# FFT convolution and spectral mixing on one core: the first transform by channel halves of one sequence, four copies of x on GpSimd, later loads, and a filter turned for two ticks at once

## The chip, the core and the metric

The kernel runs on one core of a Trainium2 chip. The metric is device time in microseconds for one launch; the median of three runs before the change is 372.04 us (372.01 to 373.72). The engines are TensorE (PE in the profile; PEld is its loading of weights), VectorE (DVE), ScalarE (ACT), GpSimd (POOL, which also issues DMAs whose f32 data is turned into f16 on the way) and SyncE (SP, which issues the other DMAs). Every engine works through its own instructions in order; engines meet at semaphores.

## What is computed

`x` has 8 sequences of 5696 positions and 128 channels, `h` one filter of 5696 positions for each channel. Each sequence is convolved with the filter, and the result goes through a spectral mixing step and a small gate:

```python
Yf = rfft(x, n=2*S, axis=1) * rfft(h, n=2*S, axis=0)[None]
x1 = irfft(Yf, n=2*S, axis=1)[:, :S, :]            # first part
X = rfft(x1, axis=1)[:, :64]                       # second part: 64 modes
Y = X mixed over channels by w_r + i*w_i, zero elsewhere
u = x1 + irfft(Y, n=S, axis=1)
out = u + relu(u @ w_ch)                           # float32
```

## The kernel before

The position is split as 64 q + p, with q from 0 to 88 (NQ = 89) and p from 0 to 63 (J = 64). The sequences are taken in four pairs. For each pair the convolution's transform has two steps, then comes the product with the filter, then the way back.

*First transform* (`a_tile`). `Xin` holds x with q on the partitions. For one channel, a matmul with the 128 columns (b, p) of the two sequences as weights and the table `F` (line 143) as the moving operand gives 180 columns: real and imaginary part for 90 frequencies k. A tile is four channels in two PSUM banks; its evacuation, scaled by 1/64, writes `As` with (b, p) on the partitions. 32 tiles make a pair. Which engine evacuates is set by lists: `SHARE` for the first pair, a turn of ACT and DVE for others, "both" for the last tile.

*Second transform* (`second`). For each k, matmuls of 64 rows each, one for each b, turn p into the second frequency, with tables `M`. A *tick* is four frequencies; there are NT = 23 ticks. The result is copied to `Xs` by ACT (`copied`) or read straight from PSUM by DVE, and DVE multiplies it with the filter into `U` (`products`), 2048 columns wide (4 x 512: two parts of the filter, two sequences, four k of 128 channels). Two ticks later (LC = 2) PE takes `U` times `Wc`, ACT copies to `Zs`, and SP stores `Zs` to memory; three ticks later (LM = 3) `modes` multiplies `Zs` with `G` for the spectral part. Tick 0 of a pair is handled apart: `second(g, 0, 0, d)` does the first 116 or 120 channels as soon as their tiles are in `As`, the rest follows, and three calls of `first_u` make its product.

*The filter.* h goes through the same first transform once (line 441: 16 tiles, `Hp` to `Ah`), with idle-time matmuls on `F` and on `Hp`, `F` between them (lines 448 to 452; their results are not used). `filter_tick` makes the second transform of four frequencies of h, evacuates it into `Hs`, and two DMAs on SP copy each half of the partitions to the other half ("turned", line 508), because the product needs both. Six filter ticks (LH = 6) stand among the first pair's tiles, the others run in the ticks of pair 0, six ahead. `filter_tick` also issues the loads of `G` at t = 1, 3, 5, 7, 9, 11.

*Loading x.* For the first pair, POOL issues 6 DMAs for h, 14 for x into `Xr`, then 6 for `M`; DVE copies x from `Xr` into `Xin` in eight pieces (`x_place`, line 364) between the evacuations of `Ah`. `Xr` lies where `Hs` will be, so `Hs` waits for these copies. For the second pair four pieces are loaded into `Xh` ahead of the first pair's tiles (line 739) and four into `Xt` in ticks; DVE places them at ticks `XPLACE`. At the border of two pairs the first six tiles of the next pair stand between the last ticks, then 26 tiles follow (line 764).

After the last pair the stored `Zs` come back, the way back from frequencies is done by matmuls with `S4` and `IBs`, and the gate and the stores of the output follow (from line 773 on).

All operations are recorded by helpers, so most rows of the trace have one line number: 323 for every matmul, 320 for every DMA, 313 and 317 for scaled evacuations by ACT and DVE, 311 and 315 for plain ones, 652 for products, 623 for those of tick 0, 365 for `x_place`. Tiles tell them apart.

Of the kernel before, what the change touches and what calls it, by code (L numbers as in the profile page):

```python
# [123 lines left out]
def bass_long_conv_fft__then__afno_spectral_mix_kernel(nc, x, h, moe_w_r, moe_w_i, moe_w_ch, out):  # L124
# [17 lines left out]
    f1 = np.zeros((P, 2 * NK))  # L142
    f1[0:NQ] = np.stack([fwd.real, fwd.imag], axis=2).reshape(NQ, 2 * NK)
# [71 lines left out]
    AW, HW, GW = NK * 2 * D, NK * D, (NK // 2 + 1) * P  # L215
    a_as = take(AW * 2)
    a_sb = at("As", AW, F16, a_as)
    XS = D + 2
    XW = 2 * J * XS
# [14 lines left out]
    DH = D // 2  # L234
    HS = DH + 2
# [7 lines left out]
    KH = [NK - 2 * XN, NK - XN]  # L243
    x_h = [at(f"Xh{i}", XB, F16, a_h + (i % 2 * HW + KH[i // 2] * D) * 2) for i in range(NXH)]
# [4 lines left out]
    f1_sb = at("F1", 2 * NK, F16, take(2 * NK * 2))  # L249
# [9 lines left out]
    a_h2, a_xt = a_h + HW * 2, a_x + 4 * S + 2 * B * P  # L259
    a_as1, a_m2 = a_as + 2 * S, a_m + 4 * S  # L260
    zt_off = [(a_h, a_h2), (a_as1, a_as1 + 2 * ZP), (a_as1 + 4 * ZP, a_as1 + 6 * ZP), (a_h + 2 * ZP, a_h2 + 2 * ZP),
# [9 lines left out]
    o_big = [a_h + 4 * ZP, a_h2 + 4 * ZP, a_st + 4 * S] + [a_g + 2 * ZP + 4096 * i for i in range(2)] + \  # L271
            [a_xt + 4096 * i for i in range(2)]
    o_off = [a_h + 4 * ZP + 4096, a_h2 + 4 * ZP + 4096, a_m2 + 2 * ZP + 4 * P, a_st + 4 * S + 4096]
# [73 lines left out]
    R.add("scalar", lambda e: e.copy(zf, ap(f1_sb, 2 * NK, J, P - J, 1, [[0, XW // 2]])), [("f1",)], [("xz",)])  # L347
# [16 lines left out]
    def x_place(i, src, toks):  # L364
        R.add("vector", lambda e: e.tensor_copy(bass.AP(x_sb, i * XN * XS, [[XW, NQ], [XS, XN], [1, D]]),  # L365
                                                src),
              list(toks) + XZ, [("xin", i)])
# [18 lines left out]
    def next_rows(c_):  # L386
        dma("gpsimd", bass.AP(x_all, QA * RA + c_ * XB, [[RA, 8], [XC * XB, 2], [1, XB]]),
            bass.AP(x.tensor, x.offset + QA * ROW + c_ * XB, [[ROW, 8], [S * D, 2], [1, XB]]), "x", (),
            [("xr", c_, 0), ("xr", XC + c_, 0)])

    def last_row(i):
        o_, w_ = i * XC // 2 * XB, XC // 2 * XB
        dma("gpsimd", bass.AP(x_all, (QA + 8) * RA + o_, [[RA, 1], [XC * XB, 2], [1, w_]]),
            bass.AP(x.tensor, x.offset + (QA + 8) * ROW + o_, [[ROW, 1], [S * D, 2], [1, w_]]), "x", (), [("xl", i)])

    for c_ in range(XC):
        if c_ == XC - 1:
            next_rows(c_)
        first_rows(0, c_)
        if c_ < XC - 1:  # L400
            next_rows(c_)
        first_rows(1, c_)
        if c_ in (0, 1):
            last_row(c_)
    XZ = [("xz",)]
    XIN = [("xin", i) for i in range(2 * XC)]
    XR = [[("xr", i, p_) for p_ in range(2)] + [("xl", i % XC // 2)] for i in range(2 * XC)]
# [19 lines left out]
    ZSLOT, DA, DF = 6, 116, 120  # L427
    ZBANK = [4, 5, 6]
    MB = 7
    WARM, LONG = 92, 22  # L430


    for i in range(WARM):
        mm(pv(6 + i % 2, 0, [[1, 2 * NK]]), f1_sb[:, 0:P], f1_sb[:, :], True, True, [("f1",)], [bank(6 + i % 2)])
# [6 lines left out]
    for j in range(16):  # L441
        t = turns("h", [0, 2, 4])
        for i in range(4):
            d = 4 * j + i
            mm(pv(t + i // 2, (i % 2) * 2 * NK, [[1, 2 * NK]]),
               ap(hp_sb, 2 * J * HS, 0, P, d, [[HS, 2 * J]]), f1_sb[:, :], True, True,
               [("hz",), ("hp", d // DC), ("f1",)], [bank(t + i // 2)])
        for i in range(4 if j < 15 else 0):
            mm(pv(6 + i % 2, 0, [[1, 2 * NK]]), f1_sb[:, 0:P], f1_sb[:, :], True, True, [("f1",)], [bank(6 + i % 2)])
# [3 lines left out]
        evac(bass.AP(ah_sb, 4 * j, [[HW, P], [DH, 2 * NK], [2, 2], [1, 2]]),  # L453
             pv(t, 0, [[1, 2 * NK], [512, 2], [2 * NK, 2]]),
             [bank(t), bank(t + 1)], [("ah", j)], 1.0 / 64,
             eng="vector" if j in (3, 7) else "scalar")
        if j % 2:
            i = j // 2 % 2 * XC + j // 4
            x_place(i, bass.AP(x_all, i * XB, [[RA, NQ], [D, XN], [1, D]]), XR[i])

# [4 lines left out]
    def a_tile(j, slots, eng=None):  # L465
        t = turns("s", slots) if len(slots) > 1 else slots[0]
        for i in range(4):
            d = 4 * j + i
            mm(pv(t + i // 2, (i % 2) * 2 * NK, [[1, 2 * NK]]),
               ap(x_sb, XW, 0, P, d, [[XS, 2 * J]]), f1_sb[:, :], True, True,  # L470
               XIN + XZ + [("f1",)], [bank(t + i // 2)])
        if eng == "both":
            for i, e in enumerate(("vector", "scalar")):
                evac(bass.AP(a_sb, 4 * j + 2 * i, [[AW, P], [D, 2 * NK], [1, 2]]), pv(t + i, 0, [[1, 2 * NK], [2 * NK, 2]]),
                     [bank(t + i)], [("as", j + i)], 1.0 / 64, eng=e, after=once(("hp", j), HP))
            return
        evac(bass.AP(a_sb, 4 * j, [[AW, P], [D, 2 * NK], [2, 2], [1, 2]]),
             pv(t, 0, [[1, 2 * NK], [512, 2], [2 * NK, 2]]),
# [10 lines left out]

    def filter_tick(t, banks):  # L490
        n = len(ticks[t])
        hb = banks
        for i, k in enumerate(ticks[t]):
            for r in range(2):
                for dh in range(2):
                    mm(pv(hb[dh], i * DH, [[1, DH]]),
                       ap(m_sb, MW, J * dh, J, k * 3 * J + (J if r == 0 else 0) + dh * J, [[1, P]]),
                       ap(ah_sb, HW, J * dh, J, (2 * k + r) * DH, [[1, DH]]), r == 0, r == 1,
                       AHT + mtok(k) + [("ag", k)], [bank(hb[dh])])
        lo, hi = KT * t * D, (KT * t + n) * D  # L500
        old = once("xr", [t_ for r_ in XR for t_ in r_]) if t == 0 else []
        for i in range(NXH):
            if KT * t + n > KH[i // 2]:
                old = old + once(("xh", i), xtok(i))
        evac(h_sb[:, lo:hi], pv(hb[0], 0, [[DH, n], [512, 2], [1, DH]]), [bank(hb[0]), bank(hb[1])], [("h", t, 0)],
             eng="scalar" if t < LH + 2 and t != 2 else "vector",
             after=old)
        for p0, p1 in ((0, J), (J, 0)):
# [457 lines left out]
```

## Time and profile before

| | |
|---|---|
| median of three runs | 372.04 us |
| span of the profiled execution | 370.1 us |
| TensorE busy | 354.7 us |
| ScalarE busy | 316.2 us |
| VectorE busy | 291.8 us |
| GpSimd busy | 75.2 us |
| first matmul on `Xin` | 27.33 us |
| first product of pair 0 | 43.43 us |

The profiled execution's own time is its span of 370.1 us, from its first to its last instruction; the device time of the runs is measured around the whole launch. A row of the timeline has start, duration, engine, line, operation, output and inputs, count, and in brackets the idle time of the engine before it with what released it. Rows of several instructions are merged, and their duration is that from first start to last end. A row of groups ends in busy time and mean ns of one, then the idle time before. A row of the DMA view ends in the size of one transfer and the median us from issue to landing. The end of a matmul is modelled, so starts are the safer figures on PE.

### The profile page before, as it was taken

The page shows a single profiled execution, that of the slowest core. Times are in us where ns is not written, and L with a number is a line of the kernel's source. Part 1 is how long each engine was busy: PE and PEld are TensorE (multiplying, and loading weights), DVE is VectorE, ACT ScalarE, POOL GpSimd, SP SyncE. Part 2 cuts the span into 40 slices and gives each one's busy share as a digit, 9 for nine tenths or more (in the row PEclk, how much of TensorE's full clock was granted, in tenths as well). Part 3 has the DMA queues.
Part 4 walks back from the last instruction along what each step waited for, and adds up shares of the span by engine and source line. Part 5 has one row for each costly group of instructions (what it writes and reads, how often), then busy time and mean ns, then how long its engine had stood idle before and what let it go on. Part 6 is the DMA issues. An engine that isn't in the chain of part 4 may idle for free.

```text
span 370.1 us, 12455 instructions
## 1 busy us (share of the span) xinstructions
PE 354.7 (96%) x5350; PEld 276.5 (75%) x5350; DVE 291.8 (79%) x332; ACT 316.2 (85%) x499; POOL 75.2 (20%) x117
## 2 busy tenths in 40 slices
PE   7999899999999999999999999999999999999994
PEld 7878766667866668866668766668899888888873
DVE  3549899988999999989999988775357777756666
ACT  8559999999999999999999999995467777688885
POOL 8804012100833311823213001151000000000000
PEclk9999999999999999999999999999999999999999
DMA  7999979969999996999996999999999999999878
GB/s 139 209 271 382 249 165 292 232 198 283 93 140 213 263 258 186 132 160 215 263 278 128 171 310 363 342 345 388 381 410 386 413 410 408 418 399 376 326 291 349
DMA packets 87048, 103.94 MB, mean 281 GB/s; under 512 B 22730, under 2 KB 72522, under 8 KB 83438
## 3 DMA queue, kind: packets, MB, share of 16 engines
q1 hardware_dynamic: 64610, 81.33, 62.5%
q0 software_dynamic: 22384, 21.83, 35.4%
q8 instruction: 42, 0.69, 0.7%
q14 instruction: 12, 0.10, 0.1%
HBM read 70.61 MB, written 51.12 MB: 329 GB/s over the span
## 4 chain that ended last, share of the span: by engine, by line
PE 78%; ACT 10%; DMA 7%; DVE 3%; issue 1%; POOL 1%; DVEq 0%; POOLq 0%
PE ps L323 78%; ACT As L313 6%; DMA out_dram<-O 5%; DMA Hin<-in_h_dram 2%; ACT R L898 1%; DVE As L317 1%; ACT Xs L311 1%; DVE U L623 1%; POOL Hin L320 1%; ACT UT L311 1%; DVE O L899 0%; ACT Zs L311 0%; DVE Hp L438 0%; ACT C L313 0%; DVE Hs L315 0%
## 5 line engine op out<-in xcount | busy, mean ns | idle before, releaser
L652 DVE TENSOR_TENSOR U<-Xs,Hs 128x2048 f16<-128x2048 f16 (+1 forms) x72 | 85.8, 1197 | 12.1 <-ACT Xs L311 11.5
L323 PE MATMUL ps<-U,Wc 128*128 128x512 f16 (+1 forms) x368 | 93.8, 376 | 1.4 <-DVE U L623 1.4
L311 ACT CAST Xs<-ps 128x1024 f16<-128x1024 f32 (+1 forms) x76 | 75.0, 995 | 5.8 <-PE ps L323 3.1
L311 ACT CAST Zs<-ps 128x512 f16<-128x512 f32 (+1 forms) x132 | 70.1, 605 | 0.7
L899 DVE TENSOR_TENSOR O<-ps,R 128x512 f32<-128x512 f32 x81 | 52.4, 684 | 21.6 <-ACT R L898 11.4
L898 ACT ACTIVATE R<-ps 128x512 f32<-128x512 f32 (+1 forms) x92 | 50.5, 592 | 8.5 <-PE ps L323 8.4
L317 DVE TENSOR_SCALAR As<-ps 128x720 f16<-128x720 f32 x64 | 53.1, 879 | 4.8 <-PE ps L323 3.3
L323 PE MATMUL ps<-As,M 64*128 64x128 f16 (+3 forms) x1504 | 52.5, 214 | 2.4 <-ACT As L313 1.2
L313 ACT ACTIVATE As<-ps 128x720 f16<-128x720 f32 (+1 forms) x68 | 48.2, 771 | 5.0 <-PE ps L323 4.8
L323 PE MATMUL ps<-F,Xin 128*128 128x180 f16 x512 | 52.1, 249 | 0.1
L323 PE MATMUL ps<-WI,UT 128*128 128x256 f16 x360 | 50.8, 278 | 0.5 <-ACT UT L311 0.4
L311 ACT CAST UT<-ps 128x712 f16<-128x712 f32 x46 | 34.5, 752 | 19.4 <-PE ps L323 18.4
L323 PEld LDWEIGHTS ps<-U,Wc 128*128 128x128 f16 x368 | 29.1, 97 | 28.2 <-DVE U L623 1.9
L323 PEld LDWEIGHTS ps<-F,Xin 128*128 128x128 f16 x512 | 45.2, 155 | 6.7 <-DVE Xin L365 0.9
L323 PEld LDWEIGHTS ps<-As,M 64*128 64x128 f16 x1504 | 42.2, 94 | 8.7 <-ACT Xs L311 1.9
L323 PEld LDWEIGHTS ps<-WI,UT 128*128 128x128 f16 x360 | 38.9, 152 | 3.2 <-issue 1.8
L323 PE MATMUL ps<-IBs,C 128*128 128x356 f16 x128 | 39.2, 314 | 0.8 <-DVE O L899 0.7
L320 POOL DMA_DIRECT2D Xt<-in_x_dram x40 | 21.4, 540 | 76.5 <-PE ps L323 76.0
L323 PEld LDWEIGHTS ps<-G,Zs 128*128 128x128 f16 x512 | 26.1, 96 | 14.1 <-ACT Zs L311 0.2
L652 DVE TENSOR_TENSOR U<-ps,Hs 128x2048 f16<-128x2048 f32 (+1 forms) x16 | 35.5, 2216 | 0.0
L323 PE MATMUL ps<-G,Zs 128*128 128x128 f16 (+2 forms) x512 | 31.9, 192 | 0.1
L311 ACT CAST Zt<-ps 128x512 f16<-128x512 f32 x52 | 29.1, 659 | 0.0
(76 smaller groups left out, 479.4 us busy)
## 6 DMA issues: line engine op xcount, KB each, us to landing
out_dram<-O SPq DMA_DIRECT2D x39, 512.0 KB, 10.5
zscr<-Zs SPq DMA_DIRECT2D x62, 256.0 KB, 6.7
zscr<-Zt SPq DMA_DIRECT2D x26, 256.0 KB, 6.6
Xt<-in_x_dram POOLq DMA_DIRECT2D x20, 320.0 KB, 6.9
W<-wscr SPq DMA_DIRECT2D x4, 1024.0 KB, 8.5
ZT0a<-zscr SPq DMA_DIRECT2D x4, 1024.0 KB, 11.0
M<-cM POOLq DMA_DIRECT2D x5, 720.0 KB, 17.6
ZT1a<-zscr SPq DMA_DIRECT2D x3, 1024.0 KB, 11.1
```

The lines of the kernel that those rows point to most:

```text
L311: R.add(e, lambda h_: h_.copy(dst, src), reads, writes, after=after)
L313: R.add(e, lambda h_: h_.activation(dst, src, COPY, scale=scale), reads, writes, after=after)
L317: R.add(e, lambda h_: h_.tensor_scalar_mul(dst, src, scale), reads, writes, after=after)
L320: R.add(eng, lambda h_: h_.dma_start(dst, src), reads, writes, ring=ring, after=after)
L323: R.add("tensor", lambda h_: h_.matmul(o, l, r, start=st, stop=sp), reads, writes)
L623: R.add("vector", lambda e: e.tensor_tensor(bass.AP(u_s[0], b * 512 + d0, [[2048, P], [1024, 2], [D, n], [1, d1 - d0]]), bass.AP(s_[0], s_ ...
L652: R.add("vector", lambda e: e.tensor_tensor(uv, src, hv, MULT), bk + [("h", t, 0), ("h", t, 1, 0), ("h", t, 1, J)], [("u", i)])
L898: R.add("scalar", lambda e: e.activation(rv, src_r, RELU), bk, [("r", i % NR)], after=once(("r", i % NR), G_ALL + XTT + [("y", 0), ("y", 1 ...
L899: R.add("vector", lambda e: e.tensor_tensor(ov, src_u, rv, ADD), bk + [("r", i % NR)], [key + (h_,)], after=once(key, old))
```

## The change

- `Xin` and `As` are laid out anew. A tile of the first transform takes four channels of each channel half of *one* sequence: 128 columns are (half, p), so tiles 0 to 15 are the first sequence and 16 to 31 the second. In the first pair a tile asks only for its own sequence's pieces (`first_pair`). In `second`, the two matmuls of a frequency are now the two channel halves; a result has the bank by half and both sequences beside each other.
- The two columns that are always zero (imaginary part of k = 0 and of k = 89) are dropped: 178 columns instead of 180, and one matmul pair less at these frequencies.
- Tick 0 of a pair is split by sequence: `second(g, 0, (0,))`, its product from PSUM, then `second(g, 0, (1,))`, a copy by ACT and its product. The two sit in banks 6, 7 and 4, 5.
- x's first DMAs come sequence by sequence, 12 instead of 14. DVE places the first sequence's four pieces during the filter's tiles; the second sequence's four pieces are copied by GpSimd, behind the DMAs that it issues.
- The filter's first transform: 2 idle-time matmuls a tile instead of 4, 4 long ones instead of 22; DVE evacuates six of the sixteen tiles instead of two.
- The six filter ticks of the first pair stand behind tiles 19, 21, 23, 25, 27, 29 instead of 11, 14, 17, 20, 23, 26.
- `Hs` is laid out for two ticks at a time from tick 6 on, and one pair of DMAs turns two ticks.
- The four loads into `Xh` move from ahead of the tiles to behind the products of ticks 0, 0, 1 and 2 of pair 0; the first placing moves from tick 3 to 4. `G` is loaded at filter ticks 5, 6, 7, 8, 9, 11.

```diff
-    f1 = np.zeros((P, 2 * NK))
+    NF = 2 * NK - 2
+    f1 = np.zeros((P, NF))
...
-    def x_place(i, src, toks):
-        R.add("vector", lambda e: e.tensor_copy(bass.AP(x_sb, i * XN * XS, [[XW, NQ], [XS, XN], [1, D]]),
+    def x_place(i, src, toks, eng="vector"):
+        R.add(eng, lambda e: e.tensor_copy(bass.AP(x_sb, i // XC * 2 * XH + i % XC * XN * HS, [[XW, NQ], [HS, XN], [XH, 2], [1, DH]]),
...
+    for b_ in range(2):
+        for c_ in range(XC):
+            first_rows(b_, c_)
+            if c_ == 0:
+                next_rows(b_)
+                last_row(b_)
...
-    ZSLOT, DA, DF = 6, 116, 120
+    ZSLOT = (6, 4)
...
-    WARM, LONG = 92, 22
+    WARM, LONG = 92, 4
...
-        for i in range(4 if j < 15 else 0):
+        for i in range(2 if j < 15 else 0):
...
-             eng="vector" if j in (3, 7) else "scalar")
-        if j % 2:
-            i = j // 2 % 2 * XC + j // 4
+             eng="vector" if j in (2, 4, 6, 9, 11, 14) else "scalar")
+        if j % 4 == 3:
+            i = j // 4
...
-    def a_tile(j, slots, eng=None):
+    def a_tile(j, slots, eng=None, first_pair=False):
+        b_ = j // 16
+        xin = XIN[b_ * XC:b_ * XC + XC] if first_pair else XIN
...
-               ap(x_sb, XW, 0, P, d, [[XS, 2 * J]]), f1_sb[:, :], True, True,
-               XIN + XZ + [("f1",)], [bank(t + i // 2)])
+               ap(x_sb, XW, 0, P, d // DH * 2 * XH + d % DH, [[HS, 2 * J]]), f1_sb[:, :], True, True,
+               xin + XZ + [("f1",)], [bank(t + i // 2)])
...
+        couple = LH <= t < NT - 1
+        if not couple or t % 2:
+            us = (t - 1, t) if couple else (t,)
+            lo = h_at(us[0])[0]
+            for p0, p1 in ((0, J), (J, 0)):
+                dma("sync", bass.AP(h_sb, p0 * 2 * HW + lo + 2 * dw, [[2 * HW, J], [1, 2 * dw]]),
+                    bass.AP(h_sb, p1 * 2 * HW + lo, [[2 * HW, J], [1, 2 * dw]]), "s", [("h", u, 0) for u in us], [("h", u, 1, p0) for u in us])
+        if t in GTICK:
...
+    GTICK = [max(LH - 1 + i, 2 * i + 1) for i in range(NG)]
...
+            product(g_, t, (ps, sl[0], 4096), bk[0], (0,))
+            second(g_, 0, (1,))
+            evac(bass.AP(x_s[e], 256, [[1024, P], [512, 2], [1, n]]), pv(ZSLOT[1], 256, [[512, 2], [1, n]]), bk[1], [("xs", e)], eng="scalar")
+            product(g_, t, (x_s[e], 0, 1024), [("xs", e)], (1,))
...
-    XPLACE = [3, 5, 7, 9, 11, 14, 17, 20], [9, 10, 13, 14, 17, 18, 20, 22]
+    XPLACE = [4, 5, 7, 9, 11, 14, 17, 20], [9, 10, 13, 14, 17, 18, 20, 22]
...
+                for e in range(NXH):
+                    if t == (0, 0, 1, 2)[e]:
+                        x_load(1, e, x_h[e], xtok(e), [("u", t)] + [t_ for r_ in XR for t_ in r_])
...
-    for i in range(NXH):
-        x_load(1, i, x_h[i], xtok(i), [t_ for r_ in XR for t_ in r_])
...
+    HTICK = [19, 21, 23, 25, 27, 29]
     for j in range(32):
-        a_tile(j, FOUR, "both" if j == 31 else SHARE[j])
-        if j >= 11 and j % 3 == 2 and (j - 11) // 3 < LH:
+        a_tile(j, FOUR, "both" if j == 31 else SHARE[j], True)
+        if j in HTICK:
             h_ = turns("s", FOUR)
-            filter_tick((j - 11) // 3, [h_, h_ + 1])
-    second(0, 0, 0, DF)
+            filter_tick(HTICK.index(j), [h_, h_ + 1])
+        if j % 4 == 1 and j < 16:
+            i = XC + j // 4
+            x_place(i, bass.AP(x_all, i * XB, [[RA, NQ], [D, XN], [DH, 2], [1, DH]]), XR[i], "gpsimd")
+    second(0, 0, (0,))
```

More of the change, by code (lines that the diff above doesn't have):

```diff
@@ L493, in filter_tick @@
         for i, k in enumerate(ticks[t]):
-            for r in range(2):
+            sk = slots(k)
+            for n_, slot in enumerate(sk):
+                r = (slot + 1) % 2 if k else 0
                 for dh in range(2):
@@ L621, in first_u @@
-    def first_u(b, s_, row, tok, d0, d1):
-        n = len(ticks[0])
-        R.add("vector", lambda e: e.tensor_tensor(
-            bass.AP(u_s[0], b * 512 + d0, [[2048, P], [1024, 2], [D, n], [1, d1 - d0]]),
-            bass.AP(s_[0], s_[1] + d0, [[row, P], [0, 2], [D, n], [1, d1 - d0]]),
-            bass.AP(h_sb, d0, [[2 * HW, P], [HW, 2], [D, n], [1, d1 - d0]]), MULT),
-              [tok, ("h", 0, 0), ("h", 0, 1, 0), ("h", 0, 1, J)], [("u", 0)])
+            sk = slots(k)
+            for n_, slot in enumerate(sk):
+                r = (slot + 1) % 2 if k else 0
+                for dh in range(2):
+                    col = k * 3 * J + (J if r == 0 else 0) + dh * J
+                    mm(pv(sl + dh, bs[0] * 256 + i * DH, [[256, nb], [1, DH]]),
+                       ap(m_sb, MW, J * dh, J, col, [[1, P]]),
+                       ap(a_sb, AW, J * dh, J, slot * D + bs[0] * DH, [[1, nb * DH]]), n_ == 0, n_ == len(sk) - 1,
+                       rd + mtok(k), [bank(sl + dh)])
@@ L766, in bass_long_conv_fft__then__afno_spectral_mix_kernel @@
                 if j == 31:
[L767 removed]
+                    second(g_ + 1, 0, (0,))
                 if wp and j % 2 == 1:
```

162 lines of the change are left out of this document (72 added, 90 removed).

## The prediction

> **What bounds the kernel now.** First the page, for busy shares; then windows by stage, to see which engine fills each; then the timeline of the first 43 us and the chain of waits over time, to see what ends each stage.
>
> ```profile
> span 370.1 us, 12455 instructions
> PE 354.7 (96%) x5350; PEld 276.5 (75%) x5350; DVE 291.8 (79%) x332; ACT 316.2 (85%) x499; POOL 75.2 (20%) x117
> ```
>
> ```profile
> 3.00:24.00 21.00, 20.19 (x221) 19.41 (x220) 9.95 (x11) 16.07 (x15) 14.02 (x24) 1.00 1.02 201
> 24.00:35.00 11.00, 10.93 (x123) 8.49 (x121) 8.16 (x11) 7.32 (x12) 4.15 (x8) 1.00 1.02 400
> 13.27:27.33 14.06, 14.03 (x146) 11.92 (x147) 8.05 (x11) 9.72 (x14) 3.75 (x6) 1.00 1.06 245
> 27.33:42.82 15.49, 14.93 (x226) 12.79 (x225) 13.70 (x17) 14.04 (x22) 4.15 (x8) 1.00 1.04 329
> 104.90:141.00 36.10, 36.10 (x559) 23.26 (x560) 34.46 (x30) 35.17 (x58) 8.33 (x16) 1.00 1.07 228
> ```
>
> Columns: window, length, busy time of PE, PEld, DVE, ACT, POOL, granted clock, DMA share, GB/s. The ticks (104.90 to 141) are full on PE, 36.10 of 36.10, with ACT close behind. From 13.27 to 27.33 PE is full too, but not with work that the result needs:
>
> ```profile
> 11.98 2.37 DVE L438 COPY Hp<-Hin 89x4096 f16<-89x4096 f16 x2 [6.71 <-DMA Hin<-in_h_dram]
> 13.27 0.53 PE L323 MATMUL ps<-F,Hp 128*128 128x180 f16 x4 [0.78 <-DVE Hp L438]
> ...
> 13.84 2.10 ACT L313 ACTIVATE Ah<-ps 128x720 f16<-128x720 f32 x3 [4.00 <-PE ps L323]
> ...
> 13.95 0.48 PE L323 MATMUL ps<-F,Hp 128*128 128x180 f16 x4
> 14.26 0.47 PE L323 MATMUL ps<-F 128*128 128x180 f16 x4
> ...
> 16.30 0.90 DVE L317 TENSOR_SCALAR Ah<-ps 128x720 f16<-128x720 f32 x1
> ...
> 19.07 5.41 ACT L313 ACTIVATE Ah<-ps 128x720 f16<-128x720 f32 x8 [0.47 <-PE ps L323]
> 19.28 0.68 DVE L365 COPY Xin<-Xr 89x2048 f16<-89x2048 f16 x1
> 22.56 0.69 DVE L365 COPY Xin<-Xr 89x2048 f16<-89x2048 f16 x1 [2.60 <-DMA Xr<-in_x_dram]
> 23.22 4.27 PE L323 MATMUL ps<-Hp,F 128*128 128x344 f16 x22
> 26.33 0.69 DVE L365 COPY Xin<-Xr 89x2048 f16<-89x2048 f16 x1 [0.81 <-DMA Xr<-in_x_dram]
> ...
> 27.33 4.68 PE L323 MATMUL ps<-F,Xin 128*128 128x180 f16 x48
> 27.84 6.24 DVE L317 TENSOR_SCALAR As<-ps 128x720 f16<-128x720 f32 x7 [0.82 <-PE ps L323]
> 28.15 4.25 ACT L313 ACTIVATE As<-ps 128x720 f16<-128x720 f32 x6 [3.67 <-PE ps L323]
> ...
> 41.27 1.96 ACT L313 ACTIVATE As<-ps 128x720 f16<-128x720 f32 x3
> ```
>
> The groups on F alone and the 22 on Hp,F are filler that writes nothing used. The filter's own transform ends near 23.2; x's transform starts at 27.33 because it asks for all eight pieces of x and the eighth lands at 26.33. So the DMA ends this stage (share 1.02, 201 GB/s while f32 is turned into f16). At a pair's border the end is set otherwise:
>
> ```profile
> 95.26 7.47 ACT As L313 x11
> 102.78 0.37 PE ps L323 x8
> ...
> 103.78 0.70 DVE U L623
> ...
> 104.58 0.27 DVE U L623
> ...
> 104.90 43.31 PE ps L323 x644
> ```
>
> Evacuations by ACT, then second, the copy, two products of tick 0, and PE is the bound again at 104.90. There are three such borders.
>
> **The change, part by part.** *x of one sequence first.* A tile now takes 4 channels of each half of one sequence, so tiles 0 to 15 need only four pieces. Half of x was in by 19.28: that copy is the fourth, and it waited for no DMA (the first four pieces are two of each sequence, the same bytes as one whole sequence; x's transfers go from 14 to 12 with the same bytes). What then ends the stage is DVE, which gets six of the sixteen evacuations of Ah (two before) besides four pieces of x. Its queue: the evacuation of tile 2 can begin when PE has done three groups of four with two fillers each. Four matmuls take 14.26 - 13.95 = 0.31, so six take 0.47, and tile 2 is ready near 13.27 + 0.94 + 0.57 = 14.8 (0.57 from the first matmul at 13.27 to its evacuation at 13.84). Then 6 x 0.90 + 4 x 0.69 = 8.15, to 22.9. PE needs 16 x 0.31 + 30 x 0.078 + 4 x 0.194 = 8.1, to 21.4; ACT 10 x 0.68 = 6.8 (5.41 / 8 each), to 20.6; both are covered. From the last copy to the first matmul on x it is 27.33 - 27.02 = 0.3. x's transform starts at 23.2 instead of 27.33: **-4.1 us**. The cut filler (4 to 2 per tile, 22 to 4) costs nothing, as it only filled that wait; if the granted clock, 1.00 in every window, fell for want of it, that would show at once. M follows x in the same queue at 400 GB/s, so its first piece (737 KB of six) is in by some 28, before the first filter tick.
>
> *GpSimd's four copies.* The trace shows no copy on POOL. The nearest rows:
>
> ```profile
> L540 POOL MEMSET ZT0b<- 32x2048 uint32 x1 | 1.8, 1794 | 21.0 <-DVE U L652 21.0
> L365 DVE COPY Xin<-Xr 89x2048 f16<-89x2048 f16 x8 | 5.4, 686 | 5.6 <-DMA Xr<-in_x_dram 5.6
> ```
>
> POOL writes 2048 elements per partition in 1.79. A copy that streams reads beside writes takes that, one that does them in turn 3.6; I take 2.0, near the row, as one pass. The bounds are 1.8 and 3.6. The second sequence lands between about 22.0 (first quarter, from 22.56) and 26.33; four copies end at 22.0 + 8.0 = 30.0, with 0.3 to PE 30.3 (POOL's DMA issues before them are over by 17, as the window from 13.27 shows 3.75 us of them and nothing after). Tile 16 is due when eight evacuations by DVE are nearly through: 23.2 + 0.5 + 8 x 0.89 (6.24 / 7) - 1.2 for the four bank pairs in flight = 29.6. **+0.7 us** of waiting, with 0 and +7.1 at the bounds; each 0.1 us of a copy is 0.4 us.
>
> The Trainium skill, "GPSIMD Engine Reference", section 3.1, gives 1.03 cycles per element where the ports bind and about 1.8 for a tight software loop, at 1.2 GHz: by the page an estimate of 1.8 or 3.1 us for 2048 elements. The memset's 1794 ns agrees with the first; no row here shows the second; by it the sum below would come to about nothing.
>
> *The filter's ticks later.* They move from tiles 11 to 26 to tiles 19 to 29, behind the copies whose memory Hs overwrites. Before, ACT had 14.04 us of work in 15.49. Now its first 16 tiles hold 8 x 0.71 (4.25 / 6) = 5.7 us of ACT against 7.1 of DVE, and all the five Hs copies come after: 8 x 0.71 + 5 x 0.59 + 0.5 = 9.1 in the second half. 7.1 + 9.1 + 0.5 to start is 16.7, against 15.9 from 27.33 to the end of its evacuations at 43.23; the four bank pairs and the wait for tile 16 let ACT catch some up: **+0.3**, bounds 0 and +0.8.
>
> ```profile
> L311 ACT CAST Hs<-ps 128x512 f16<-128x512 f32 x7 | 4.1, 589 | 0.0
> ...
> L313 ACT ACTIVATE As<-ps 128x720 f16<-128x720 f32 x64 | 46.6, 787 | 5.0 <-PE ps L323 4.8
> L311 ACT CAST Zs<-ps 128x512 f16<-128x512 f32 x124 | 67.7, 619 | 0.7
> ```
>
> *Turned for two ticks; next x and G later.* Turning in couples takes 16 of SP's 46 transfers of Hs away and no work from PE. Its early transfers landed late while the next pair's x moved:
>
> ```profile
> Hs<-Hs SPq DMA_DIRECT2D x4, 64.0 KB, 9.3
> ...
> Hs<-Hs SPq DMA_DIRECT2D x4, 64.0 KB, 2.6
> ...
> G<-cG SPq DMA_DIRECT2D x1, 256.0 KB, 4.0
> ...
> 48.90 0.69 PE L323 MATMUL ps<-G,Zs 128*128 128x128 f16 x8
> ...
> Xt<-in_x_dram POOLq DMA_DIRECT2D x1, 320.0 KB, 6.0
> ...
> 51.51 1.21 DVE L652 TENSOR_TENSOR U<-Xs,Hs 128x2048 f16<-128x2048 f16 x1
> ```
>
> 9.3 is for issues at 36.8 to 39.7, 2.6 for those at 46.5 to 49.6. The turned filter of tick 0 is issued some 5 us before its product, so it fits by the second and not by the first; moving next x behind the product of tick 0 makes the second likely. G's first part comes out of SP after the sixth filter tick, near 40.5, and lands near 45 (4.0 and the issue); the modes that read it follow the last evacuation (41.27 + 1.96 = 43.23 before, 40.1 after) as before by 48.90 - 43.23 = 5.7, at 45.8. Its margin is under 1 us. Next x: tick 0's product ends near 42 (40.1 and the 0.37, 0.59 and 0.70 of a border with their hops); POOL then issues two transfers of 0.5 us per piece with only later loads queued behind them, and the first piece lands at 42.5 + 6.0 = 48.5 or later. DVE asks for it ahead of tick 4's product, which was at 51.51 and comes to 48.4. Behind DVE's wait stand the products, for which PE waits two ticks later. **+0.5 us** for both, bounds 0 and +2.
>
> *Borders.* Product and second of tick 0 split by sequence instead of by channel: the leftover of 0.27 and the hops about it go (104.90 - 104.48 = 0.4). ACT, 35.17 of 36.10 busy just behind, gives part back: 3 x -0.35 = **-1.05**, bounds 0 and -1.3. The first product now takes 1024 elements out of PSUM where it took 928; DVE does it while ACT still evacuates and copies, so 0. The modes now wait for both halves of a Zs, but come a tick after them: 0. The four matmuls fewer per pair (two rows of zeros gone) are 0.1 us each pair, left out. Rows of 178 instead of 180 columns: 720 to 712 elements take 1.1% off 7.47 at three borders and off some 11 us of the first: **-0.3**.
>
> *Shapes.* A product's filter is read in runs of 256 instead of 512, a Zs copy writes runs of 64 instead of 128, x is placed in runs of 64. As is written in runs of 2 at 787 / 720 = 1.09 ns per element, Zs in runs of 128 at 1.21: short runs are not dearer. 0; if a Zs copy lost 2%, ACT's slack of 0.93 in 36.10 would still cover most of it (36 such copies in the window, 0.4 us).
>
> Sum: -4.1 + 0.7 + 0.3 + 0.5 - 1.05 - 0.3 = **-3.95**. On the profiled execution the span of 370.1 becomes 366.15; the median of the runs, 372.04, lies 1.94 above that span for what surrounds it, so 368.1.
>
> **Rivals.** *Slow copies (the other side).* If POOL needs 3.6 per copy, tile 16 waits until 22.0 + 14.4 + 0.3 = 36.7, 6.4 us more than in the sum: 374.5. For it: no copy on POOL is in the trace, and all 16 tiles of the second sequence hang on the fourth. Against: 1.79 for as many elements written. It decides from 3.0 us per copy (2.0 + 3.95 / 4), where the sum is nil.
>
> *DVE's copy shut out.* If a POOL copy that has begun keeps DVE's fourth copy of x (due at 22.2) from starting until it ends, tile 0 comes up to 1.4 us later: 369.5. For it: both are due near 22; against: POOL's data may land later than DVE's turn. "SBUF", section "Who interferes with whom", of the Trainium skill states such a lock for copies on VectorE in its fast modes. No row here has both at work on copies.
>
> *The head start is lost in pair 0.* If the turned filter, G or next x lands late, PE, first in first out, stops in ticks 0 to 5; at the bound of 2, that is 1.5 more than in the sum: 369.6. For it: 9.3 us above and the two thin margins; against: the load that made the 9.3 has moved.
>
> **How the numbers follow.** Forecast 0.52 (its own range 366.0 to 369.5), shut-out copy 0.14, loss in pair 0 0.14, slow copies 0.20. About 0.5%, 1.9 us, is what a measurement tells from no change. Faster by more than that is below 370.2: nearly all of the first and two thirds of the second and third, 0.70; no change has the rest of those and copies of up to 3.5 us, 0.16; slower 0.14. The range runs from 365.0, copies of 1.8 with the full gain at the borders and no late transfer, to 373.0, copies of some 3.2 us.
>
> **What would show it.** In the changed profile: the first matmul on Xin at about 23.2, after a DVE copy of x that waited for no DMA; four POOL copies of some 2.0 us, a gap of under 1 us on PE before tile 16; the first border's W matmul 0.35 us nearer to its last evacuation; products at 1219 ns and Zs copies at 619 as before. POOL copies over 3 us, or PE idle at G or Hs in the first ticks, would make it wrong.

## The result, and the profile after

The changed kernel takes 374.58 us (median of 22 runs, 371.79 to 379.41) against 372.05 for the kernel before (22 runs, 371.20 to 374.19): a ratio of 1.0053 with the interval 1.0037 to 1.0069, slower by half a per cent. The medians here and below count every run; the ratios leave out runs of over 1.5% above the fastest of their kernel, two of these 22 of the changed one. The forecast was 368.1, and its range ended at 373.0.

The profiled execution is the changed kernel's fastest, 371.79 us, with a span about as long as before. So two things need a cause: a start that came out as forecast and brought nothing in this execution, and a median 2.8 us above it. First the page: span and busy times.

```profile
span 370.0 us, 12251 instructions
PE 347.0 (94%) x5274; PEld 268.9 (73%) x5274; DVE 291.6 (79%) x328; ACT 312.5 (84%) x495; POOL 81.6 (22%) x119
```

TensorE (PE) has 7.7 us less to do, mostly the filler that was cut, and the span is the same: it idles longer. The timeline of the start (start, length, engine, line, what, count, and in brackets the idle time before and what ended it) shows that this is not where it idles:

```profile
22.03 0.68 DVE L370 COPY Xin<-Xr 89x2048 f16<-89x2048 f16 x1
...
22.77 6.32 PE L328 MATMUL ps<-F,Xin 128*128 128x178 f16 x64 [0.38 <-DVE Xin L370]
23.11 7.43 POOL L370 COPY Xin<-Xr 89x2048 f16<-89x2048 f16 x4 [7.67 <-DMA Xr<-in_x_dram]
...
30.59 1.47 PE L328 MATMUL ps<-F,Xin 128*128 128x178 f16 x16 [1.50 <-POOL Xin L370]
...
39.09 1.16 ACT L318 ACTIVATE As<-ps 128x712 f16<-128x712 f32 x2
...
42.33 3.16 POOL L325 DMA_DIRECT2D Xh<-in_x_dram  x6 [11.80 <-DVE U L648]
...
43.33 1.04 PE L328 MATMUL ps<-U,Wc 128*128 128x512 f16 x4
```

x's transform starts at 22.77 instead of 27.33. GpSimd's four copies take 7.43 us, 7.43 / 4 = 1.86 each. PE waits 1.50 us for the last of them. The last evacuation ends at 39.09 + 1.16 = 40.25 instead of 43.23, and the first matmul of a tick on W starts at 43.33. In the timeline of the kernel before that one stood here:

```profile
46.27 1.04 PE L323 MATMUL ps<-U,Wc 128*128 128x512 f16 x4
```

So 2.94 us are won at 43. The windows of after behind it (length; busy PE, PEld, DVE, ACT, POOL; granted clock, DMA share, GB/s) show where they go; the second line ends at the first evacuation of XT, which closes pair 0, and the third holds one pair's ticks, as a window of before did in the prediction.

```profile
39.71:43.33 3.62, 2.02 (x78) 1.63 (x79) 2.49 (x4) 3.03 (x6) 1.00 (x2) 1.00 0.43 104
43.33:93.77 50.44, 45.81 (x842) 30.30 (x839) 41.48 (x49) 43.70 (x69) 8.05 (x15) 1.00 0.95 249
106.30:142.00 35.70, 35.54 (x554) 22.76 (x555) 34.00 (x30) 34.79 (x58) 8.37 (x16) 1.00 1.08 229
```

The same stretch of before, from its first matmul on W to its first evacuation of XT:

```profile
46.27:91.86 45.59, 45.55 (x846) 30.63 (x843) 41.43 (x49) 43.87 (x69) 4.39 (x8) 1.00 0.91 233
```

PE has nearly the same work, 45.8 and 45.6 us. Before, it idles for 0.04 us of the stretch; after, for 4.63. The clock is 1.00 in both. The loss lies in pair 0 alone: from pair 1 on the ticks are nearly full again (35.54 of 35.70). The groups of waits of after between 40 and 95 us (who waited at which line for whom; total, times, longest) say what for:

```profile
PEld ps L328 <- DVE Hs L320: 5.5, 6, 2.7
...
PE ps L328 <- DVE Hs L320: 4.3, 5, 2.6
DVE U L648 <- DMA Hs<-Hs: 3.8, 2, 3.4
...
DVE Xin L370 <- DMA Xh<-in_x_dram: 1.1, 2, 0.6
```

VectorE's product (L648) waits for a turned filter half (third line); behind it in VectorE's queue stands its copy of a later filter tick out of PSUM (L320), for whose bank PE waits (first two lines). The timeline has the longest of these stops on both engines:

```profile
61.54 1.23 DVE L648 TENSOR_TENSOR U<-Xs,Hs 128x2048 f16<-128x2048 f16 x1 [3.37 <-DMA Hs<-Hs]
...
63.43 0.41 PE L328 MATMUL ps<-Ah,M 64*128 64x64 f16 x16 [2.56 <-DVE Hs L320]
```

Two links of the chain of waits are transfers of this kind, and SP's timeline shows a queue that stood still: it took 7.00 us to issue two of them, from 48.23, and the slowest of all landed 13.0 us after its issue.

```profile
44.38 8.62 DMA Hs<-Hs
...
59.53 6.54 DMA Hs<-Hs
```

```profile
48.23 7.00 SPq L325 DMA_DIRECT2D Hs<-Hs  x2
```

Why they are late is seen in the DMA's share (the next to last column) in windows of 2 us, and in the median from issue to landing by stretch of issue (33 to 41.8, 41.8 to 45, 45 to 48.15, 48.15 to 54 us, the last column):

```profile
36.00:38.00 2.00, 2.00 (x48) 1.76 (x44) 1.87 (x3) 2.00 (x5) 0.00 (x0) 1.00 0.66 183
38.00:40.00 2.00, 1.66 (x41) 1.31 (x39) 1.68 (x4) 2.00 (x5) 0.00 (x0) 1.00 0.30 75
40.00:42.00 2.00, 1.20 (x56) 1.03 (x58) 1.59 (x2) 1.52 (x4) 0.00 (x0) 1.00 0.41 105
...
46.00:48.00 2.00, 2.00 (x45) 1.36 (x44) 1.93 (x3) 2.00 (x4) 1.03 (x2) 1.00 1.00 201
```

```profile
Hs<-Hs SPq DMA_DIRECT2D x12, 64.0 KB, 2.9
...
Hs<-Hs SPq DMA_DIRECT2D x2, 128.0 KB, 8.3
...
G<-cG SPq DMA_DIRECT2D x2, 256.0 KB, 12.1
...
Hs<-Hs SPq DMA_DIRECT2D x2, 128.0 KB, 10.5
```

With next x held back until tick 0's product, the DMA is some two thirds empty from 38 to 42, where its share was 1.09 and 1.08 before. Then next x, the couples, G's parts and the rows of Zs are asked for together, and a turned couple needs 8 to 10 us where a single half had needed 2.9. It isn't its size: in the kernel below that turns each tick by itself, halves of 64 KB issued from 46 to 56 land after 9.9 and 10.3 us.

At the first border the chain of waits goes from the last evacuation, ending at 101.39 + 3.15 = 104.54, through one copy and one product to the first matmul on W at 106.46, 1.92 us instead of 104.90 - 102.73 = 2.17:

```profile
101.39 3.15 ACT As L318 x5
...
104.58 0.40 PE ps L328 x14
...
105.00 0.59 ACT Xs L316
...
105.62 0.70 DVE U L648
...
106.46 5.82 PE ps L328 x93
```

### The profile page after: what moved, and what is told of

Same layout as the page of the kernel before. It is cut to its first block, busy times and chain, and to the rows that moved or that the text cites. A ratio compares the mean times of both kernels' runs of the same rounds, so it can differ in the third digit from the quotient of the medians.

```text
span 370.0 us, 12251 instructions
## 1 busy us (share of the span) xinstructions
PE 347.0 (94%) x5274; PEld 268.9 (73%) x5274; DVE 291.6 (79%) x328; ACT 312.5 (84%) x495; POOL 81.6 (22%) x119
## 4 chain that ended last, share of the span: by engine, by line
PE 68%; DMA 10%; ACT 10%; POOL 4%; DVE 3%; SPq 2%; issue 2%; DVEq 0%; POOLq 0%
PE ps L328 67%; ACT As L318 7%; DMA Hs<-Hs 4%; DMA Xr<-in_x_dram 4%; DMA Xt<-in_x_dram 2%; POOL Xin L370 2%; SPq L325 2%; DVE U L648 1%; ACT R L914 1%; POOL Xr L325 1%; POOL Hin L325 1%; DVE Hs L320 1%; DVE Xin L370 1%; ACT Xs L316 0%; DVE As L322 0%
## 5 line engine op out<-in xcount | busy, mean ns | idle before, releaser
L648 DVE TENSOR_TENSOR U<-Xs,Hs 128x2048 f16<-128x2048 f16 (+1 forms) x76 | 88.6, 1171 | 17.6 <-ACT Xs L316 12.4
L322 DVE TENSOR_SCALAR As<-ps 128x712 f16<-128x712 f32 x64 | 52.8, 874 | 5.9 <-PE ps L328 4.4
L328 PE MATMUL ps<-F,Xin 128*128 128x178 f16 x512 | 51.5, 249 | 2.8 <-POOL Xin L370 1.5
L328 PE MATMUL ps<-As,M 64*128 64x128 f16 (+1 forms) x1480 | 50.1, 215 | 2.9 <-ACT As L318 2.4
L318 ACT ACTIVATE As<-ps 128x712 f16<-128x712 f32 (+1 forms) x68 | 47.6, 764 | 4.3 <-PE ps L328 4.1
L328 PEld LDWEIGHTS ps<-As,M 64*128 64x128 f16 x1480 | 40.4, 94 | 8.4 <-ACT As L318 2.9
L648 DVE TENSOR_TENSOR U<-ps,Hs 128x2048 f16<-128x2048 f32 (+1 forms) x20 | 40.4, 2018 | 0.0
L328 PEld LDWEIGHTS ps<-G,Zs 128*128 128x128 f16 x512 | 25.3, 96 | 14.8 <-ACT Zs L316 3.9
```

Of the source, the lines that this page charges most:

```text
L318: R.add(e, lambda h_: h_.activation(dst, src, COPY, scale=scale), reads, writes, after=after)
L322: R.add(e, lambda h_: h_.tensor_scalar_mul(dst, src, scale), reads, writes, after=after)
L328: R.add("tensor", lambda h_: h_.matmul(o, l, r, start=st, stop=sp), reads, writes)
L648: R.add("vector", lambda e: e.tensor_tensor(uv, sv, hv, MULT), bk + [("h", t, 0), ("h", t, 1, 0), ("h", t, 1, J)], [("u", i)])
```

## The experiments

Each group ran on one chip beside its own runs of the kernel before. A median stands beside its ratio to those, with the interval.

**The changed kernel again** (no edit), for a second profile.

> The changed kernel once more, for a second profile and for the spread of its time. Theory A (the next pair's x, asked for at ticks 0 to 2, fills the DMA engines just while pair 0 turns its filter, so turned halves land too late and PE stops in ticks 5 to 11): 373.5 to 375.5, and a profile in which PE's idle time between 47 and 70 us is 5 to 9 us, more than the 4.9 of the first profile, all of it behind Hs. Rival B (the couple itself is late: a transfer of two ticks waits for the second tick and is twice as large): the same time, the same place. Rival C (the new shapes cost something in every tick): idle or longer rows in pairs 1 to 3 too.

374.32 us, 1.0068 (1.0022 to 1.0114). In this execution PE waits for G instead. Its timeline and its windows:

```profile
48.58 0.48 PE L328 MATMUL ps<-G,Zs 128*128 128x128 f16 x8 [2.33 <-DMA G<-cG]
...
49.97 1.89 PE L328 MATMUL ps<-U,Wc 128*128 128x512 f16 x4
```

```profile
46.00:48.00 2.00, 0.25 (x2) 0.00 (x0) 1.66 (x2) 1.46 (x3) 1.04 (x2) 1.00 1.00 278
48.00:50.00 2.00, 1.42 (x41) 1.16 (x42) 0.56 (x1) 0.00 (x0) 1.04 (x2) 0.88 1.05 236
50.00:52.00 2.00, 2.00 (x12) 0.89 (x11) 1.60 (x3) 1.65 (x3) 0.00 (x0) 0.50 1.07 252
52.00:54.00 2.00, 2.00 (x41) 1.37 (x39) 1.37 (x3) 1.01 (x2) 0.00 (x0) 0.77 1.11 268
```

So not all of PE's idle time stands behind Hs, as was expected. Which late transfer stops PE differs between the two executions, and behind the stop the granted clock (third from the end) falls to 0.50: four matmuls on W take 1.89 us instead of 1.04. The first 22 runs of the changed kernel fit this: the fastest has a mean clock of 0.999, the other 21, at 373.39 us or more, have 0.980 to 0.995; the kernel before, in the groups below, has 0.995 to 1.000. But the clock doesn't order single executions: of these five the fastest, 370.91 us, has 0.992 and the profiled one, 373.32, 0.994.

**Next x early again, in the changed kernel.**

> The changed kernel, with the four loads of Xh issued behind GpSimd's copies, near 30.6 us, instead of at ticks 0 to 2. Theory A: the DMA engines are used between 36 and 44 us, where the changed kernel left them at a share of 0.3 to 0.6, and the ticks from 5 on no longer wait: 4 to 7 us less than the changed kernel, minus 0 to 2.5 us for turned halves of ticks 0 and 1 that now land later: 368 to 371. Rival B: the couples still wait: 373 to 375. Rival C: 373 to 375.

```diff
+        if j == 14:          # loop over the 32 tiles, behind GpSimd's copies
+            for e in range(NXH):
+                x_load(1, e, x_h[e], xtok(e), [t_ for r_ in XR for t_ in r_])
...
-                    if t == (0, 0, 1, 2)[e]:
-                        x_load(1, e, x_h[e], xtok(e), ...)
```

372.19 us, 1.0005 (0.9976 to 1.0034), 2.1 below the changed kernel beside it. The intervals of these two overlap; from the changed kernel's first 22 runs (1.0037 to 1.0069) it is just clear. Part of the loss goes, not all, and less than was expected: now the first turned halves are late (VectorE waits 3.7 us for them), as the 9.3 us of before foretold, and G still is (1.4).

**Each tick turned by itself, in the changed kernel.**

> The changed kernel, with each tick turned by itself from tick 6 on, as before the change, and next x and G still late. Rival B: the waits for Hs go, 367.5 to 369.5. Theory A: a tick's half is issued one tick sooner but SP issues 16 transfers more into the same crowd: 373 to 376. Rival C: 374 to 375.

```diff
-        if t < LH or t == NT - 1:     # where a tick lies in Hs
+        if True:
...
-        couple = LH <= t < NT - 1
+        couple = False
```

374.47 us, 1.0069 (1.0031 to 1.0107): the same as the changed kernel. Turning for two ticks at once is not the cause.

**Next x late, in the kernel before**: this one move and nothing else of the change.

> The kernel before, with only the four loads of Xh moved to ticks 0, 0, 1, 2 (and the first placing from tick 3 to 4), as the change has them. Theory A: the move alone costs here too, PE waits for Hs or the placing in ticks 4 to 11: 374 to 378 against 372.0. Rivals B and C: no cost, or a small gain as the early turned halves land sooner: 371 to 372.5.

```diff
+                    if t == (0, 0, 1, 2)[e]:
+                        x_load(1, e, x_h[e], xtok(e), ...)
...
-    XPLACE = [3, 5, 7, 9, 11, 14, 17, 20], ...
+    XPLACE = [4, 5, 7, 9, 11, 14, 17, 20], ...
...
-    for i in range(NXH):
-        x_load(1, i, x_h[i], xtok(i), [t_ for r_ in XR for t_ in r_])
```

375.55 us (four runs), 1.0121 (1.0085 to 1.0157): 4.0 us slower than before. The profile, of the fastest of the four, has the same chain of waits as the changed kernel:

```profile
PEld ps L323 <- DVE Hs L315: 4.0, 7, 1.4
...
PE ps L323 <- DVE Hs L315: 2.8, 5, 1.2
```

This shows the first cause: in the kernel before, holding next x back costs, on its own, more than the 2.94 us that the earlier start brings. In the changed kernel, taking it back regains 2.1.

**G early, and next x early or in the middle**: four kernels. G early is `GTICK = [2 * i + 1 for i in range(NG)]`; next x in the middle issues one piece behind each of the tiles 22, 24, 26 and 28, while the first pair's filter ticks still run.

> The changed kernel with only G's loads back at filter ticks 1, 3, 5, 7, 9, 11. Theory A (what counts is how much has to pass the DMA engines between tick 0 and tick 10; next x is most of it): three of six parts of G move into the slack before tick 0, so a little is won, 372.5 to 374. Rival D (G behind twelve turns on SP is itself the late one): PE's wait for G goes and the time falls to 370 to 372.

> Next x behind GpSimd's copies, near 30.6 us, and G at ticks 1, 3, 5: the loads as before the change, with its head start. Theory A: the turned halves of ticks 0 to 2 land 9 us after issue, as in the profile of before, and the head start of 3 us is too short for that: 370.5 to 372.5, with PE or DVE waiting 2 to 4 us for Hs in ticks 0 to 3. Rival D: the wait for G was what was left, 368.5 to 370.

> Next x one piece at a time behind tiles 22, 24, 26 and 28 (36 to 39 us), where the changed kernel leaves the DMA engines at 0.3 to 0.7, and G at ticks 1, 3, 5. Theory A: the first turned halves land before the crowd, next x is through before tick 5: no waits for Hs in ticks 5 to 11, most of the head start is kept: 367.5 to 370.5. Rival D: the same as the run with next x at 30.6, within 1 us.

> The same with G as late as in the change. Theory A: G lands in the crowd of next x and PE waits 1 to 3 us for it at tick 3: 369.5 to 372. Rival D: more, 372 to 374. If G's place does not matter: as the run with G early.

```diff
-    GTICK = [max(LH - 1 + i, 2 * i + 1) for i in range(NG)]
+    GTICK = [2 * i + 1 for i in range(NG)]
...
+        if j in (22, 24, 26, 28):
+            e = (22, 24, 26, 28).index(j)
+            x_load(1, e, x_h[e], xtok(e), [("as", j)] + [t_ for r_ in XR for t_ in r_])
```

The rows late with late and early with late are of the group above, the other four of a group of their own, so ratios are to be compared here, not medians.

| next x | G | us | ratio (interval) |
|---|---|---|---|
| late | late (changed kernel, second runs) | 374.32 | 1.0068 (1.0022 to 1.0114) |
| late | early | 373.53 | 1.0024 (0.9991 to 1.0057) |
| early | late | 372.19 | 1.0005 (0.9976 to 1.0034) |
| early | early | 372.33 | 0.9991 (0.9957 to 1.0025) |
| middle | late | 374.62 | 1.0053 (1.0011 to 1.0094) |
| middle | early | 371.09 | 0.9973 (0.9949 to 0.9997) |

With next x in the middle G decides: the two intervals don't meet. Late, PE stands still for it, and early it doesn't; from the timeline of the kernel with both in the middle and late:

```profile
49.73 0.48 PE L328 MATMUL ps<-G,Zs 128*128 128x128 f16 x8 [3.53 <-DMA G<-cG]
```

The two kernels differ by 3.5 us in the median. With next x early, G's place makes no difference that can be told (0.9991 and 1.0005): the turned halves are late either way. The best of the six is 0.27% faster than before, slower than was expected (367.5 to 370.5), and PE still waits 1.8 us in it for VectorE's copies of Hs. In its profile the clock falls as well, this time behind the wait for GpSimd's last copy; its timeline and a window:

```profile
30.71 2.44 PE L328 MATMUL ps<-F,Xin 128*128 128x178 f16 x16 [1.73 <-POOL Xin L370]
```

```profile
32.00:34.00 2.00, 2.00 (x25) 1.65 (x24) 0.90 (x1) 1.58 (x4) 0.00 (x0) 0.50 1.02 426
```

The 16 matmuls take 2.44 us where the changed kernel's profile has 1.47 behind a wait of 1.50. Whether this fall holds the kernel back is what the next runs were for.

**Filler in the gap ahead of tile 16**, 20 products on F, in the changed kernel and in the best so far; and the best so far with 6 of them and the last of the four copies done by VectorE.

> The changed kernel with 20 filler matmuls on F ahead of tile 16, in the bank that tile 16 then overwrites, so that PE works while GpSimd's copies end. Theory E (PE's wait of 1.5 us there, after a stage with less filler, lets the granted clock fall to 0.5 for some 4 us in part of the executions): no window between 28 and 40 us below a clock of 0.99 any more, and 0.5 to 1.5 us off the median: 372.8 to 374.2; drops behind the waits for Hs stay. If the clock does not matter: 374 to 375.

> Next x behind tiles 22 to 28, G at ticks 1, 3, 5, and the filler ahead of tile 16. Theories A and E together: clock 0.99 or more from 28 to 60 us, first matmuls of tick 0's second half near 40.3 instead of 41.7, 1 to 2 us under the same kernel without filler: 369 to 370.5. If the clock does not matter: 370.5 to 371.5.

> The same with 6 fillers, and the last of the second sequence's pieces copied by VectorE (0.68 us) instead of GpSimd (1.86): GpSimd's three end near 28.7, so PE's wait ahead of tile 16 goes from 1.5 to under 0.5 us; VectorE's evacuations lose 0.7. 0.5 to 1 us under the run before it: 368.5 to 370. If VectorE is the bound of these tiles: the same time.

```diff
+        if j == 16:
+            for i in range(20):
+                mm(pv(b16, 0, [[1, NF]]), f1_sb[:, 0:P], f1_sb[:, :], True, True, [("f1",)], [bank(b16)])
...
-            x_place(i, ..., XR[i], "gpsimd")
+            x_place(i, ..., XR[i], "vector" if j == 13 else "gpsimd")
```

377.63 us, 1.0160 (1.0127 to 1.0194); 375.40, 1.0078 (1.0050 to 1.0106); 371.97, 0.9989 (0.9957 to 1.0021): all three above what was expected. The gap was filled and the clock stayed at 1.00 there, yet the first two lost 3 us and more far behind, in the last stage, which nothing had touched. The timeline of the second:

```profile
252.29 1.80 PE L328 MATMUL ps<-XT,W 128*128 128x64 f16 x56
256.80 0.37 PE L328 MATMUL ps<-XT,W 128*128 128x64 f16 x8 [2.71 <-issue]
```

PE stops in the middle of one group of 64 matmuls and waits for nothing that the profile names ("issue"); then the clock falls to 0.50 there too. The kernel with 6 products has a like stop of 1.48 us. The theory that the filler would pay was wrong as tried, and a second question stood open: the filler, or 20 instructions more?

**The same 20 products elsewhere.** 112 instead of 92 products at the very start of the changed kernel; the kernel with next x in the middle, G early and the filler, with 72 instead of 92 at the start; and that kernel without filler, the last copy done by VectorE.

> The changed kernel with 112 filter products instead of 92 at the very start, where they run before the first rows of h have landed, and nothing else. Theory of the program's place (the waits of 2.7 to 3.1 us for nothing the profile shows, in the last stage of the two kernels with 20 products more ahead of tile 16, come of the 20 instructions that TensorE's program is longer, wherever they stand): such a wait of 2.5 to 3.1 us shows again behind 245 us, and the median is 376 to 378 us. Rival (it comes of what the fillers do at 29 to 31 us): no such wait, and the median is that of the changed kernel, 373.5 to 375 us, or up to 1.5 us more if the first products on h wait for the longer start.

> The kernel with next x behind tiles 22 to 28, the early G and 20 products ahead of tile 16, with 20 products fewer at the start, so that TensorE's program behind tile 16 is as long as in the kernel without them. Theory of the program's place: no wait of over 1.5 us for nothing behind 245 us; with the gap ahead of tile 16 filled the granted clock stays above 0.95 from 28 to 42 us and the median is 369.5 to 371 us, 1 us below the kernel without fillers. Rival (the fillers themselves cost the last stage): the wait of 2.7 us is there and the median is 375 us again.

> Next x behind tiles 22 to 28, the early G, and the last of the four later pieces copied by VectorE, with no filler: TensorE's program is as long as the changed kernel's. Theory of the program's place: the 1.5 us wait for nothing of the kernel with 6 fillers is gone, and the median is 370 to 371.5 us. Rival (that wait has another cause): 371.5 to 372.5 us as with the 6 fillers.

```diff
-    WARM, LONG = 92, 4
+    WARM, LONG = 112, 4        # 72 in the second
```

The first takes 378.25 us, 1.0171 (1.0148 to 1.0195), though its 20 products run before any data has come, and its timeline has the same stop:

```profile
256.82 1.39 PE L328 MATMUL ps<-XT,W 128*128 128x64 f16 x42
...
260.63 0.38 PE L328 MATMUL ps<-XT,W 128*128 128x64 f16 x9 [2.42 <-issue]
```

The second, with the filler but a program that behind tile 16 is as long as without it, has no wait for nothing of over 0.6 us behind 245 and takes 370.97, 0.9979 (0.9954 to 1.0004). So the stop comes with how many instructions stand ahead of it in TensorE's program, not with what the 20 do. A longer program is not in itself the cause: the kernel before has 76 matmuls more than the changed one and no such stop.

The traces say more. In all four kernels that have the stop (three with 20 products more, one with 6) it stands ahead of the 3798th or 3799th matmul of the program, whatever that one does, and it ends 1.25 to 1.45 us after a DMA packet of 16 KB that the trace calls "instruction" (in the kernel of the timeline of 252.29 above, from 254.57 to 255.51). The kernels that add no products wait at this matmul too, but for 0.65 us at most. So TensorE most likely waits there for the next piece of its own program; no run tried that by itself, and why the piece is so late only in these four stays open.

The second shows a price of its shorter start as well: PE stops for 3.44 us ahead of the first product on Hp. Its windows:

```profile
12.00:14.00 2.00, 0.87 (x6) 0.88 (x7) 2.00 (x2) 0.01 (x1) 2.00 (x2) 0.59 1.04 172
14.00:16.00 2.00, 2.00 (x16) 2.00 (x15) 0.45 (x2) 1.52 (x2) 1.38 (x3) 0.50 1.04 199
16.00:18.00 2.00, 2.00 (x16) 2.00 (x14) 1.72 (x3) 0.76 (x1) 0.00 (x0) 0.50 1.10 221
```

That execution, the slowest of its twelve, starts x's transform some 3 us later for it. The third takes 370.90 us, 0.9975 (0.9954 to 0.9995), 1.2 us below before and level with the best of the six: some two fifths of the 2.94 us, and only with next x and G put back to earlier places. Its program is as long as the changed kernel's, and the wait of 1.5 us for nothing that the kernel with 6 products had is gone. The clock stays at 1.00 at tile 16, and yet it is no faster than the best of the six. Its waits between 40 and 95 us show that a late turned half is still there, and the clock falls with it, at 47.64:

```profile
PE ps L328 <- DVE Hs L320: 2.4, 1, 2.4
```

## Why the prediction was wrong

**Start of x's transform**, -4.1 forecast: -4.56 measured (27.33 to 22.77). VectorE's queue set it, as worked out.

**GpSimd's copies**, +0.7: 1.86 us each against 2.0, near the lower bound of 1.8, but the second sequence's first piece was ready for GpSimd at 23.11 and not at 22.0, so the copies ended at 30.54 instead of 30.0, and tile 16, due at 29.09 instead of 29.6, waited 1.50. The price was nearly right, the landing time was the term that was off most. The Trainium skill, "GPSIMD Engine Reference", section 3.1, gives 1.03 cycles per element where ports bind, an estimate of 1.76 us here; the trace agrees within 6%. The rival of a shut-out copy did not arise: VectorE's fourth copy ended at 22.71, before GpSimd's first began.

**Filter ticks bunched**, +0.3: the transform's last evacuation, with everything ahead of it, ended at 40.25 against 40.1.

**"Turned for two ticks; next x and G later"**, +0.5 with bounds 0 and +2: this is the step that failed. From the first matmul on W to the last evacuation of the next border it is 104.54 - 43.33 = 61.21 us against 102.73 - 46.27 = 56.46, +4.75. The rival of a head start lost in pair 0 named the place and the queue rightly and priced it at 1.5 more than the sum; it was given 0.14. The prediction took the 9.3 and 2.6 us of the turned halves as with and without next x beside them, and priced three first landings: tick 0's half, G's first part and next x's first piece. The halves turned in the ticks, from tick 6 on, it put at nothing. But they, G's later parts and the rows of Zs go through the same stretch, and what had been loaded from 36 to 48 us was now loaded behind 42.

These halves were what stopped PE in the first profile: 4.3 of its 4.63 us of idle time stand behind VectorE's copies of Hs. In the second it was G, whose margin of under 1 us failed: SP got to it at 42.38 instead of 40.5, its first part landed 6.1 us later, and PE went on at 48.58 instead of 45.8. Its price of 4.0 us had been read from an issue at 49.6 to 50.2, behind the crowd; two parts issued from 36 to 41 had taken 9.1 in the same profile of before. The right reading of before was the DMA's share by window, and the whole list of what was due in it and when. Measured one by one, next x held back costs 4.0 us in the kernel before, and G later costs 3.5 with next x in the middle. One part of the change was not taken back alone: the filter's six early ticks, which stand later too.

**The cut filler**, "costs nothing": in both profiles of the changed kernel the granted clock did not fall at the start, and x's transform began early. What was not priced is the clock behind the stops that the change brings later, ahead of tile 16 and in pair 0. One fall lasts 3.41 us (last section), so it costs at most 1.7; by the mean clocks, 0.980 to 0.995 against 0.999, the other 21 executions had some one to four of them, an estimate. That is enough for the 2.8 us of the median above the profile, but no run took the fall away by itself in pair 0, and in the kernel that turns each tick by itself executions at 0.999 and 0.992 took 374.47 and 372.14. So its share is not settled.

**Borders**, three times -0.35: -0.25, -0.33 and -0.24, measured from last evacuation to first matmul on W. From the first border's last evacuation to the third's, however, 106.0 us before became 106.1 (102.73 to 208.74; 104.54 to 210.68): what the borders gave did not add up to a gain over the two pairs. Of it, 0.74 us went again at 196, where PE waits for the placing of a piece of the next pair's x that landed late, which it didn't before.

**Shapes**, 0: right. Groups of after:

```profile
L648 DVE TENSOR_TENSOR U<-Xs,Hs 128x2048 f16<-128x2048 f16 x69 | 83.8, 1220 | 16.5 <-ACT Xs L316 11.4 <-DMA Hs<-Hs 3.8 <-PE ps L328 0.5
...
L316 ACT CAST Zs<-ps 128x512 f16<-128x512 f32 x124 | 67.6, 623 | 2.2 <-PE ps L328 2.0
```

1220 and 623 ns against 1219 and 619.

The profiled execution ends level all the same, because its last stage, from the third border's last evacuation on, is 2.0 us shorter (370.0 - 210.68 = 159.3 against 370.1 - 208.74 = 161.4). The chain of before goes there through a wait for a store:

```profile
320.68 16.68 DMA out_dram<-O
```

The chain of after has none. No part of the change aims at it, and the second profile of the changed kernel has 160.1, so it is not counted as a gain: that the profiled span came out level was luck, as far as is known.

## What to carry to other kernels

Before a load is moved out of the way of others, list by window what else the DMA has to land behind it: idle share given up early was not had back later here, and small transfers behind a crowd landed some three times as late (9.9 and 10.3 us for 64 KB against 2.9). A gain at a stage's start is safe only if what the next stage needs moves up as much; here the best kernels issue next x and G earlier than the change did. When only a few instructions are added or cut on the bounding engine, measure a kernel of the same program length beside it.

## What the runs showed of the hardware

The granted clock changed only on a grid of 3.41 us, which starts elsewhere in each execution: in all sixteen traces the times between two changes are multiples of it, and a fall to 0.50 lasted 3.41 us (15 times) or 6.83 (twice). The windows of the changed kernel's second profile add up to one: (1.00 - 0.88) x 2 / 0.5 + 2 + (1.00 - 0.77) x 2 / 0.5 = 3.4. What counts is how much of one step of the grid TensorE idles. From the clock's first rise to 360 us, all ten steps at full clock with an idle share of over 0.52 were followed by a fall, of eleven from 0.47 to 0.51 seven, and none below (the shares are worked out from matmul ends, which are modelled). So a stop of 1.73 us within one step lowered the clock (best of the six kernels), one of 2.56 that lay across two, with 0.38 and 0.42 of them idle, did not (changed kernel, first profile), and three gaps of 0.49 to 0.65 us in one step did in three kernels. The Trainium skill, "TensorE: Matmul & The Clock Gate", Part 1, has half clock after at least one idle window of some 3.4 us. The half and the length agree, but a window half idle was enough here.

Twenty matmuls more at either of two places ahead on TensorE brought a stop of 2.4 to 3.0 us 230 to 250 us later, inside a group of equal matmuls, and with the slower clock behind it went with 3 to 4 us more in the changed kernel. With 20 fewer elsewhere the stop was gone, and each time it ended 1.25 to 1.45 us after a 16 KB packet of kind "instruction".
